# Chunk pairs of T3's inner products 0,2 with 1,3; the first half's sums all made in the gated stage; B21 of pair 0 ahead of pair 1's, with one load of a rest fewer

## The chip, the cores and the metric

The kernel runs on one core of one Trainium2 chip. The metric is the device time of one execution in microseconds (us); lower is better. A profile of one execution lies beside the times: it records when each instruction ran on each engine (PE for matrix products, DVE and ACT for elementwise work, POOL and SP for issuing transfers), what ended each wait, and what the transfers moved.

## What is computed

The reference mixes two branches of one layer with a learned gate per token (x is 2048 tokens of 640 features, the hidden width of the gated branch is 1536, there are 32 heads of 20):

```python
g = sigmoid((x * gate_w).sum(-1, keepdims=True))
a = A(x, wqkv, wo)                     # linear attention: phi(q) (phi(k)^T v) / (phi(q) . sum phi(k)), then @ wo
b = (sigmoid(x @ w_gate) * (x @ w_up)) @ w_down
return g * a + (1 - g) * b
```

The kernel folds the attention's `phi(k)^T v` and `wo` into one matrix, so that the scaled `phi(q)` and the gated hidden values are one long input of a single last product with `w_down` and that matrix stacked under each other.

## The kernel before

**Arithmetic.** Every f32 operand is split into a high and a low part (ACT writes the high part, DVE the low one: `split`), and each product of tiles is three matmuls, one at `L203` and two at `L205` (`mm3`). A matmul over 512 columns starts every 0.227 us when nothing is waited for. On top of that the products are Strassen-Winograd products of 2x2 blocks, which is where the many names come from.

**Stages.** The k projection and the attention's sums come first (to about 155 us), then the q projection, then the *gated stage* from about 222 to 513 us: a loop over `f` of 0 to 11, one block of 128 hidden features per turn, 24.5 us each, for two token pairs (pair 1 is token groups 2 and 3, pair 0 groups 0 and 1; a group has 512 tokens). Last comes the *output stage* from 513 us to the end.

**What the gated stage leaves.** For each pair it writes seven forms of the last product's input to DRAM (`h_dram[pr, name]`, names `B11 B21 T2 T1 T3 B22 T4`). Each form has 8 *chunks* of 128 rows by 512 tokens: chunks 0 to 5 come from the twelve hidden blocks (chunk `p` from `f` of `2p` and `2p+1`, stored in the turn after), chunks 6 and 7 from `phi(q)`. A ninth, shorter piece, the *rest* (`r_dram[pr]`), is left over because the length is odd.

**T3's second level.** The product with T3 is a Winograd product itself, with seven inner products P1 to P7. Its two contraction halves, A and B, are sets of chunks; `u` of 0 and 1 (the *first* and the *second half* of the sets) tells which two of the four chunks of a set are meant: `KA[u]` and `KB[u]`. Its input needs sums over DRAM, made by transfers of 512 KB that POOL issues. Those that add into their target (`accum_op`) are called *adds* below.
- `f_copy(u)`, line 1384: `f_sum` gets pair 1's A. `f_add(u, 0, KA)`, line 1387, adds pair 0's A: that is P7's input.
- `f_add(u, 0, KB)` adds pair 0's B to it in place: P6's input. `f_add(u, 1, KB)` adds pair 1's B: P3's input. As all three stand in the same place of `f_sum`, P6's add must wait until P7 has been read, and P3's until P6 has been read; `load_h` arranges that in the output stage (`F_DUE`).
- `f_low(u)`, line 1391, adds pair 0's B into its A: P5's input.

**The output stage.** `HQ` lists 62 inputs in order, each two chunks of a form (512 KB) read by SP; `jobs` runs over that list. An input takes 18, 12 or 6 matmuls (6 for an inner product), that is 4.1, 2.7 or 1.4 us. `next_h` reads into one of five raw tiles (three named `hw`, two `ws`, of which the latter also carry weights), `queue_h` splits into one of five tiles `hf`; a raw tile is free again when its split is done, and an `hf` tile when the products of the input five places before are done. The weights (`wa`; SP reads them through `ws`) are split in the same stage: kinds E, O, L, S, and I for the inner products (`("wa", "I", u)` for the two halves). The weights and inputs are put in the order of ACT and DVE by `Order`, which keeps estimated clocks of PE, ACT and DVE, and by `plan`. `load_rest(pr)` reads the rest of a pair into two tiles `ot` and splits them into `hr` (two instructions each of ACT and DVE); it is called at the places in `plan` and `REST_AT`, after so many finished inputs (`done_h`). `hr` is there once, so the rest of pair 1 takes the place of that of pair 0.

**What sets the order around the change.** SP and POOL each issue their transfers strictly in program order, and a waiting transfer holds back all behind it. In the program, a POOL transfer also waits for the landing of the POOL transfer eight places before it. In the gated stage `hooks[f]` runs once per turn, after the third step of both pairs' blocks. Tiles `c` (six with tag `c11`, six with `c12`) hold the results of a turn until POOL's stores of them have landed; ACT's first results of turn 11 take over tiles that the stores of T2 of turns 8 and 9 free.

Of the kernel before, what the change touches and what calls it, by code (L numbers as in the profile page):

```python
# [7 lines left out]
F32 = mybir.dt.float32  # L8
# [3 lines left out]
OP = mybir.AluOpType  # L12
# [3 lines left out]
P = 128  # L16
# [4 lines left out]
TG = 512  # L21
# [148 lines left out]
def a_cost(w):  # L170
    return 0.19 + w * 0.00084


def v_cost(w):
    return 0.155 + w * 0.00104
# [3 lines left out]
def gated_mix_kernel(ctx: ExitStack, tc: tile.TileContext, xt, xn, wk, wv, wo, wst_q, wst_f, out_t):  # L179
    nc = tc.nc  # L180
# [4 lines left out]
    dram = ctx.enter_context(tc.tile_pool(name="scratch", bufs=1, space=DRAM))  # L185
    order = Order()
# [10 lines left out]
    def ps_tile(tag):  # L197
        return psum.tile([P, 512], F32, name=tag, tag=tag, bufs=2)

    def mm3(out, l_hi, l_lo, r_hi, r_lo, first, last, left=False, whole=None):  # L200
        lows = [(l_hi, r_lo), (l_lo, r_hi)]
        o, r = (out, r_hi) if whole is None else whole
        nc.tensor.matmul(o, l_hi, r, start=first, stop=False, skip_group_check=True)  # L203
        for n, (a, b) in enumerate(lows[::-1] if left else lows):
            nc.tensor.matmul(out, a, b, start=False, stop=last and n == 1, skip_group_check=True)  # L205
# [51 lines left out]
    h_dram = {(pr, n): dram.tile([P, FC // 2 + 2, TG], F32, name=f"h{pr}{n}") for pr in range(2) for n in FORMS}  # L257
# [1 line left out]
    f_dram = dram.tile([P, TG], F32, name="f_dram")  # L259
    z_dram = dram.tile([32, D], F32, name="z_dram")  # L260
    s_dram = dram.tile([P, FC // 2 + 2, 2 * TG], F32, name="s_dram")
    f_sum = dram.tile([P, 4, TG], F32, name="f_sum")
    r_dram = [dram.tile([P, 2, TG], F32, name=f"r{pr}") for pr in range(2)]
    bdn = HPG * DH

# [37 lines left out]
    class XForms:  # L303
# [3 lines left out]
        def __init__(self, pool):  # L307
            self.fb, self.fr, self.fa = (self.pair(pool, *a) for a in ((3, "b"), (3, "r"), (2, "a")))
# [546 lines left out]
    for c in range(1, 4):  # L855
        ck = chunks[c]
        if c == 1:
            a, b = KPlain(2), KPlain(3)
# [15 lines left out]
        else:  # L874
            a, b = KBlock(2 * c), KBlock(2 * c + 1)
# [401 lines left out]
    for n, b in enumerate(blocks):  # L1277
        nxt = blocks[n + 1] if n + 1 < len(blocks) else None
# [98 lines left out]

    PP = (FC // 2 + 2) // 2

    KA, KB = (slice(0, 2), slice(2, 7, 4)), (slice(3, 5), slice(5, 8, 2))  # L1380
    KF = (slice(0, 2), slice(2, 4))

    def f_copy(u):
        nc.gpsimd.dma_start(f_sum[:, KF[u]], h_dram[1, "T3"][:, KA[u]])

    def f_add(u, pr, c):
        nc.gpsimd.dma_start(f_sum[:, KF[u]], h_dram[pr, "T3"][:, c[u]], accum_op=OP.add)

    def f_low(u):
        h = h_dram[0, "T3"]  # L1390
        nc.gpsimd.dma_start(h[:, KA[u]], h[:, KB[u]], accum_op=OP.add)
# [159 lines left out]
    def den_all():  # L1551
        order.need(("den", 1), False)
        queue_s()

    hooks = {0: begin, 3: den_all, 5: lambda: f_copy(0), 6: lambda: f_add(0, 0, KA), 11: lambda: f_low(0)}
    NH = 5
    WA, WI, RAW = {}, {}, {}

# [121 lines left out]
    def whole(pr, n):  # L1680
        return [(pr, n, pp) for pp in range(PP)]

    def mixed(text):

        out, at = [], {}
        for n in text.split():
            key = (1 if n.endswith("+") else 0, n.rstrip("+"))
            out.append((*key, at.get(key, 0)))
            at[key] = at.get(key, 0) + 1
        return out  # L1690

    HQ = [(pr, "B11", pp) for pp in range(PP) for pr in (1, 0)]
    HQ += whole(1, "B21") + whole(1, "T4") + whole(0, "B21")
    HQ += mixed("T2+ T2+ P7 T2+ P7 T2+ P1 T2 P1 T2 P6 T2 P6 T2 P5 P5 T1+ P2 T1+ P2 T1+ P3 P3 T1+")
    HQ += mixed("B22+ P4 B22+ P4 B22+ B22+") + whole(0, "T1") + whole(0, "B22") + whole(0, "T4")
    INNER = {"P7": (f_sum, KF), "P6": (f_sum, KF), "P3": (f_sum, KF), "P1": (h_dram[1, "T3"], KA),
             "P2": (h_dram[1, "T3"], KB), "P5": (h_dram[0, "T3"], KA), "P4": (h_dram[0, "T3"], KB)}
    F_DUE = {}
    HF, HR = {}, {}
# [7 lines left out]
    def load_h(k, tiles=None):  # L1707
        if k < len(HQ):
            pr, n, pp = HQ[k]
            if n in INNER:  # L1710
                d, c = INNER[n]
                if (n, pp) in F_DUE:
                    F_DUE.pop((n, pp))()
                src = d[:, c[pp]]
            else:
                src = h_dram[pr, n][:, 2 * pp:2 * pp + 2]
            if tiles:
                for i, t in enumerate(tiles):
                    nc.sync.dma_start(t, src[:, i])
            else:  # L1720
                if RING[k] == "hw":
                    tiles = PL["hb"].tile([P, 2, TG], F32, name="hw", tag="hw", bufs=3)
                else:
                    tiles = PL["hb"].tile([P, 2 * D], F32, name="ws", tag="ws", bufs=2)[:, :2 * TG].rearrange("p (i c) -> p i c", i=2)
                nc.sync.dma_start(tiles, src)
            HR[k] = tiles, max(order.pe, order.vec) + (5.0 if k < 5 else 8.0)
            nxt = {"P7": ("P6", 0, KB), "P6": ("P3", 1, KB)}.get(n)
            if nxt:
                key = nxt[0], pp
                F_DUE[key] = lambda: f_add(pp, *nxt[1:])  # L1730
                order.late.append((HR[k][1], lambda: F_DUE.pop(key, int)()))
# [13 lines left out]
        if k < len(HQ):  # L1745
            order.add(a_cost(2 * TG), v_cost(2 * TG), whole, ("h", k), lambda: HR[k][1] if k in HR else 1e9)

    REST, REST_AT = {}, {13: 0, 20: 1, 50: 0}
    F_AT = {20: lambda: f_low(1)}

    def load_rest(pr):

        t = [out_tile() for _ in range(2)]
        for i in range(2):
            nc.sync.dma_start(t[i], r_dram[pr][:, i])

        def fn(i):
            if i == 0:
                REST[pr] = PL["hb"].tile([P, 2, 2, TG], F32R, name="hr", tag="hr")
            split(REST[pr][:, 0, i], REST[pr][:, 1, i], t[i])  # L1760
        for i in range(2):
            order.add(a_cost(TG), v_cost(TG), lambda i=i: fn(i), ("r", pr), lambda at=order.pe + (8.0 if done_h < 13 else 11.0): at, lazy=True)

    turn = 0
    fb = {f: [FBlock(pr, f) for pr in (1, 0)] for f in range(FC)}
# [7 lines left out]
    for f in range(FC):  # L1773
        cur, nxt, old = fb[f], fb.get(f + 1, ()), fb.get(f - 1, ())
# [70 lines left out]
    def out_tile():  # L1845
        return PL["hb"].tile([P, TG], F32, name="ot", tag="ot", bufs=8)
# [8 lines left out]
    for _ in range(3):  # L1855
# [3 lines left out]
    plan = [("E", 1), ("h", 2), ("h", 3), ("E", 2), ("h", 4), ("E", 3), ("h", 5), ("O", 0),  # L1859
            ("h", 6), ("O", 1), ("h", 7), ("O", 2), ("h", 8), ("O", 3), ("h", 9), ("L", 0)]  # L1860
    plan += [("S", p) for p in range(2 * PP)] + [("I", u) for u in range(2)]
    for k in range(10, len(HQ)):
        plan.append(("h", k))
        if k == 12:
            plan.append(("r", 1))
    done_h = 0

    def advance():
# [132 lines left out]
    class Inner:  # L2001
# [3 lines left out]
        def __init__(self, n):  # L2005
            self.n = n
            if n == "P7":
                IB["t"] = ps_tile("ch")
            elif n == "P1":
                IB["u"] = ps_tile("ch")  # L2010
            x = {"P2": (1, 0), "P3": (1, 1), "P4": (0, 0)}.get(n)
            self.dst = X[x[0]][x[1]] if x else IB["u" if n in ("P1", "P5") else "t"]
            self.first = n in ("P7", "P1", "P5")

        def product(self, u, h):
            w = WI[self.n, u]
            prod(self.dst, [(w[:, 0, i], w[:, 1, i], h[:, 0, i], h[:, 1, i]) for i in (0, 1)], self.first and u == 0)

        def out(self):
            n = self.n  # L2020
# [28 lines left out]
    for k, q in jobs:  # L2049
        pr, n, pp = HQ[k]  # L2050
        if (pr, n) not in passes:
            passes[pr, n] = Inner(n) if n in INNER else Pass(pr, n)
        b = passes[pr, n]
        order.need(("h", k))
        if n in INNER:
            if q is None:
                order.need(("wa", "I", pp))
                b.product(pp, HF[k])
                if pp == 1:
                    b.out()  # L2060
        else:
            order.need(("wa", b.kind, pp))
            if b.ek == "E":
                order.need(("wa", "E2", pp))
            b.product(q, pp, HF[k])
            if pp == PP - 1:
                b.rest(q)
                b.out(q)
        if q is None:
            done_h = k + 1  # L2070
            if done_h in REST_AT:
# [54 lines left out]
```

## Time and profile before

| what | us |
|---|---|
| time, median of 3 runs (lowest, highest) | 731.04 (730.49, 731.05) |
| the profiled execution's own time | 732.2 |
| its span, first to last instruction | 730.5 |
| PE busy in the span | 719.8 |
| DVE, ACT, POOL busy | 504.1, 330.9, 139.3 |
| granted PE clock over the span | 0.999 |

The profiled execution took 1.2 us more than the median run; 1.7 us of its time lie outside the span. PE is busy for 98.5% of the span, so the figures to look for are its few waits. How to read the rows that follow: in the view over time, a row is *start, length, engine, line, operation, out<-in*, then how many instructions it merges, and in brackets how long the engine was idle before it and what ended that. In a table of windows a row has the length of the window, each engine's busy time with its instructions in parentheses, the granted PE clock, the busy share of the 16 DMA engines and what they moved in GB/s. In a list of transfer issues the last number is the median time from issue to landing in us.

### The profile page before, as it was taken

To read this page: it belongs to the slowest core of one execution; us is meant where nothing else is said; L and a number is where in the kernel's file an instruction comes from. 1 tells how busy PE (TensorE), PEld (TensorE's weight loads), DVE (VectorE), ACT (ScalarE), POOL (GpSimd) and SP (SyncE) were. 2 spreads that over 40 slices of the span, in tenths; PEclk is the share of its full clock that TensorE was granted. 3 is DMA by queue.
4 is the path that set the end of the run, shared out by engine and by line. 5 is a ranking of instruction groups with operands and counts; after the bars stand their busy time and mean duration, and the time that the engine had idled before them with its cause. 6 is when DMAs were issued, how large, how long until landed. Compare 5 with 4: busy or idle time off the path is not lost.

```text
span 730.5 us, 9634 instructions
## 1 busy us (share of the span) xinstructions
PE 719.8 (99%) x3399; PEld 605.8 (83%) x3399; DVE 504.1 (69%) x807; ACT 330.9 (45%) x563; POOL 139.3 (19%) x231
## 2 busy tenths in 40 slices
PE   9999999999999999999999999999999999899998
PEld 8998998878888888888888888888888887688786
DVE  4878576768773688678879688777768686764330
ACT  5664637267766233333333233324367565642321
POOL 0311011122530023213223222341200021010000
PEclk9999999999999999999999999999999999999999
DMA  8553535897545474556589748476988899986401
GB/s 249 138 139 72 162 55 146 206 288 253 198 159 194 152 226 130 176 195 242 215 256 327 248 182 280 174 262 207 357 276 285 297 268 294 296 281 197 166 30 72
DMA packets 64165, 152.45 MB, mean 209 GB/s; under 512 B 7887, under 2 KB 24431, under 8 KB 64118
## 3 DMA queue, kind: packets, MB, share of 16 engines
q1 hardware_dynamic: 43477, 91.65, 39.0%
q0 software_dynamic: 20496, 60.07, 27.2%
q8 instruction: 26, 0.43, 0.2%
q14 instruction: 22, 0.17, 0.1%
q10 hardware_dynamic: 144, 0.13, 0.1%
HBM read 98.20 MB, written 55.08 MB: 210 GB/s over the span
## 4 chain that ended last, share of the span: by engine, by line
PE 86%; DMA 6%; DVE 3%; ACT 3%; issue 1%; SPq 0%; DVEq 0%; ACTq 0%
PE ch L205 17%; PE rot L205 15%; PE cc L205 14%; PE dd L205 11%; PE ch L203 8%; PE rot L203 7%; PE cc L203 7%; PE dd L203 5%; DMA hw<-h0T 2%; DMA hw<-h1T 1%; ACT hf L215 1%; DMA wo_sb<-wo 1%; DMA xst<-xt 1%; DMA zacc<-kb 1%; PE rot L301 1%
## 5 line engine op out<-in xcount | busy, mean ns | idle before, releaser
L219 DVE TENSOR_TENSOR hf<-hw,hf 128x1024 fp32r<-128x1024 f32 x45 | 54.7, 1223 | 29.9 <-ACT hf L215 29.5
L219 DVE TENSOR_TENSOR c<-cc,c 128x512 f32<-128x512 f32 x56 | 37.7, 686 | 46.1 <-PE cc L205 40.5
L205 PE MATMUL ch<-hf,wa 128*128 128x512 f32 x192 | 59.3, 390 | 1.6 <-DVE hf L219 1.6
L215 ACT ACTIVATE hf<-hw 128x1024 fp32r<-128x1024 f32 x45 | 47.2, 1056 | 29.0 <-PE rot L205 20.6
L205 PE MATMUL dd<-hf,wa 128*128 128x512 f32 x144 | 44.3, 389 | 0.0
L205 PEld LDWEIGHTS ch<-hf,wa 128*128 128x128 f32 x192 | 35.8, 188 | 9.6 <-DVE hf L219 2.2
L215 ACT ACTIVATE wG<-wst 128x640 fp32r<-128x640 f32 x17 | 12.4, 737 | 65.0 <-PE dd L205 65.0
L215 ACT ACTIVATE c<-ch 128x512 f32<-128x512 f32 x32 | 19.1, 597 | 48.7 <-PE ch L205 43.9
L205 PE MATMUL rot<-hf,wa 128*128 128x512 f32 x128 | 39.4, 389 | 0.0
L203 PE MATMUL ch<-hf,wa 128*128 128x512 f32 x96 | 37.7, 393 | 0.6 <-ACT hf L215 0.4
L1849 POOL DMA_DIRECT2D out_t<-ot x18 | 9.9, 552 | 145.1 <-DVE ot L219 142.2
L203 PE MATMUL dd<-xrh,wG 128*128 128x512 f32 x90 | 35.3, 393 | 0.0
L205 PE MATMUL dd<-xrh,wG 128*128 128x512 f32 x90 | 35.1, 390 | 0.0
L205 PE MATMUL dd<-xrl,wG 128*128 128x512 f32 x90 | 35.0, 389 | 0.0
L219 DVE TENSOR_TENSOR hf<-ws,hf 128x1024 fp32r<-128x1024 f32 x15 | 18.3, 1223 | 23.2 <-ACT hf L215 23.1
L219 DVE TENSOR_TENSOR c<-c,om 128x512 f32<-128x512 f32 x48 | 33.1, 692 | 1.6
L203 PE MATMUL cc<-xbh,wS 128*128 128x512 f32 x84 | 32.7, 389 | 0.0
L205 PE MATMUL cc<-xbl,wS 128*128 128x512 f32 x84 | 32.7, 389 | 0.0
L205 PE MATMUL cc<-xbh,wS 128*128 128x512 f32 x84 | 32.7, 389 | 0.0
L205 PE MATMUL cc<-hf,wa 128*128 128x512 f32 x104 | 32.1, 390 | 0.3 <-DVE hf L219 0.3
L205 PEld LDWEIGHTS dd<-hf,wa 128*128 128x128 f32 x144 | 27.0, 188 | 5.6
L215 ACT ACTIVATE c<-rot 128x512 f32<-128x512 f32 x24 | 14.2, 597 | 38.1 <-PE rot L205 30.8
(486 smaller groups left out, 2149.0 us busy)
## 6 DMA issues: line engine op xcount, KB each, us to landing
hf<-p_dram SPq DMA_DIRECT2D x16, 512.0 KB, 4.8
wst<-wst_f SPq DMA_DIRECT2D x12, 640.0 KB, 4.6
hw<-h1T SPq DMA_DIRECT2D x13, 512.0 KB, 6.7
xst<-xt SPq DMA_DIRECT2D x10, 640.0 KB, 8.9
h1T<-c POOLq DMA_DIRECT2D x24, 256.0 KB, 3.0
h0T<-c POOLq DMA_DIRECT2D x24, 256.0 KB, 4.4
xnst<-xn SPq DMA_DIRECT2D x16, 320.0 KB, 3.2
p_dram<-qr POOLq DMA_DIRECT2D x20, 256.0 KB, 2.8
```

The source lines that it names most:

```text
L203: nc.tensor.matmul(o, l_hi, r, start=first, stop=False, skip_group_check=True)
L205: nc.tensor.matmul(out, a, b, start=False, stop=last and n == 1, skip_group_check=True)
L215: nc.scalar.activation(out, src, fn, **kw)
L219: nc.vector.tensor_tensor(out, a, b, op=op)
L301: nc.tensor.matmul(wps[:, :w], ones_w[:, :P], ones_w[:, :w], start=True, stop=True)
L1849: (eng or nc.gpsimd).dma_start(out_t[o * P:(o + 1) * P, g * TG + c0:g * TG + c1], t[:, c0:c1])
```

## The change

It has five parts.
1. The sets of chunks of T3's inner products: A was chunks 0,1 and 2,6 and B was 3,4 and 5,7; now A is 0,2 and 4,6 and B is 1,3 and 5,7. So the first half needs only chunks 0 to 3, which are there after turn 7 of the gated stage. The first half's A and B are now two strips per row rather than one.
2. `f_sum` has 8 places rather than 4: P7, P6 and P3 have places of their own for the first half, and the second half stays in one place. All adds of the first half are issued in the gated stage (`hooks` 7 to 11): P7's copy and add, two more copies of it (P6, P3), `f_low(0)`, two adds of pair 0's B, one of pair 1's B. That is two copies and one add more than before in all.
3. P7 of the second half is read before that of the first, and only the second half's adds of P6 and P3 are issued in the output stage. `f_low(1)` comes after 10 inputs rather than 20.
4. B21 of pair 0 comes ahead of B21 and T4 of pair 1. So the rest of pair 0 is needed first, then that of pair 1, then that of pair 0 again: three loads rather than four.
5. The splits of the second and the third rest are forced at a fixed place (`done_h` of 15 and 52); before, that of the third was forced only by the product that uses it.

```diff
-    f_sum = dram.tile([P, 4, TG], F32, name="f_sum")
+    f_sum = dram.tile([P, 8, TG], F32, name="f_sum")
...
-    KA, KB = (slice(0, 2), slice(2, 7, 4)), (slice(3, 5), slice(5, 8, 2))
-    KF = (slice(0, 2), slice(2, 4))
-
-    def f_copy(u):
-        nc.gpsimd.dma_start(f_sum[:, KF[u]], h_dram[1, "T3"][:, KA[u]])
-
-    def f_add(u, pr, c):
-        nc.gpsimd.dma_start(f_sum[:, KF[u]], h_dram[pr, "T3"][:, c[u]], accum_op=OP.add)
+    KA, KB = (slice(0, 3, 2), slice(4, 7, 2)), (slice(1, 4, 2), slice(5, 8, 2))
+    KF = {n: (slice(2 * i, 2 * i + 2), slice(6, 8)) for i, n in enumerate(("P7", "P6", "P3"))}
+
+    def f_copy(u, n="P7"):
+        nc.gpsimd.dma_start(f_sum[:, KF[n][u]], h_dram[1, "T3"][:, KA[u]] if n == "P7" else f_sum[:, KF["P7"][u]])
+
+    def f_add(u, pr, c, n="P7"):
+        nc.gpsimd.dma_start(f_sum[:, KF[n][u]], h_dram[pr, "T3"][:, c[u]], accum_op=OP.add)
...
-    hooks = {0: begin, 3: den_all, 5: lambda: f_copy(0), 6: lambda: f_add(0, 0, KA), 11: lambda: f_low(0)}
+    def f_copies():
+        f_copy(0, "P6")
+        f_copy(0, "P3")
+
+    def f_lows():
+        f_low(0)
+        f_add(0, 0, KB, "P6")
+        f_add(0, 0, KB, "P3")
+
+    hooks = {0: begin, 3: den_all, 7: lambda: f_copy(0), 8: lambda: f_add(0, 0, KA), 9: f_copies,
+             10: f_lows, 11: lambda: f_add(0, 1, KB, "P3")}
...
-            out.append((*key, at.get(key, 0)))
-            at[key] = at.get(key, 0) + 1
+            i = at[key] = at.get(key, -1) + 1
+            out.append((*key, 1 - i if n == "P7" else i))
...
-    HQ += whole(1, "B21") + whole(1, "T4") + whole(0, "B21")
+    HQ += whole(0, "B21") + whole(1, "B21") + whole(1, "T4")
...
-            nxt = {"P7": ("P6", 0, KB), "P6": ("P3", 1, KB)}.get(n)
+            nxt = {"P7": ("P6", 0, KB), "P6": ("P3", 1, KB)}.get(n) if pp else None
...
-    REST, REST_AT = {}, {13: 0, 20: 1, 50: 0}
-    F_AT = {20: lambda: f_low(1)}
+    REST, REST_AT = {}, {13: 1, 50: 0}
+    F_AT = {10: lambda: f_low(1)}
...
-            plan.append(("r", 1))
+            plan.append(("r", 0))
...
-            if done_h == 30:
-                order.need(("r", 1), False)
+            if done_h in (15, 52):
+                order.need(("r", int(done_h == 15)), False)
```

POOL in the gated stage, turn 10 (in these rows `h0T` with number 77 is T3 of pair 0, `f_sum` the sums; rows with `hf` are stores of the scaled `phi(q)`, rows with `c` stores of turn 9's results):

```order
 L1491 DMA h0T_75<-hf 128x512
 L1491 DMA h0T_79<-hf 128x512
+L1391 DMA h0T_77<-h0T_77 128x2x512
+L1387 DMA f_sum<-h0T_77 128x2x512 x2
 L1337 DMA h1B_85<-c 128x512
 L1337 DMA h0B_78<-c 128x512
```

Three adds now stand between the stores of `phi(q)` and the stores of turn 9, which are behind them on the same queue.

POOL at the end of the gated stage and in the output stage (`out_t<-ot` are stores of finished outputs; the rows above the first add are the last stores of T3 and T4 of pair 0):

```order
 L1337 DMA h0T_77<-c 128x512
 L1337 DMA h0T_79<-c 128x512
-L1849 DMA out_t<-ot 128x512 x3
-L1387 DMA f_sum<-h0T_77 128x1024
-L1849 DMA out_t<-ot 128x512
+L1391 DMA h0T_77<-h0T_77 128x2x512
+L1859 DMA out_t<-ot 128x512 x6
 L1387 DMA f_sum<-h0T_77 128x2x512
-L1849 DMA out_t<-ot 128x512 x2
-L1391 DMA h0T_77<-h0T_77 256x1x512
-L1387 DMA f_sum<-h1T_84 128x1024
 L1387 DMA f_sum<-h1T_84 128x2x512
```

Of five adds in the output stage three stay, and `f_low(1)` now stands ahead of the first output, right behind the last stores of the gated stage.

ACT near the end (`hr<-ot` is the split of a rest, `hf` of an input, `ot<-dd` an output of T1 of pair 0, which is the product that uses this rest):

```order
 L215 ACTIVATE ot<-rot 128x512
 L215 ACTIVATE hf<-ws 128x1024
 L215 ACTIVATE hf<-hw 128x1024
-L215 ACTIVATE hf<-ws 128x1024
-L215 ACTIVATE hf<-hw 128x1024
 L215 ACTIVATE hr<-ot 128x512 x2
+L215 ACTIVATE hf<-hw 128x1024 x2
 L215 ACTIVATE ot<-dd 128x512 x2
```

The split of the rest has moved ahead of two splits of inputs.

More of the change, by code (lines that the diff above doesn't have):

```diff
@@ L1687, in mixed @@
             key = (1 if n.endswith("+") else 0, n.rstrip("+"))
-            out.append((*key, at.get(key, 0)))
-            at[key] = at.get(key, 0) + 1
+            i = at[key] = at.get(key, -1) + 1
+            out.append((*key, 1 - i if n == "P7" else i))
         return out
     HQ = [(pr, "B11", pp) for pp in range(PP) for pr in (1, 0)]
-    HQ += whole(1, "B21") + whole(1, "T4") + whole(0, "B21")
+    HQ += whole(0, "B21") + whole(1, "B21") + whole(1, "T4")
     HQ += mixed("T2+ T2+ P7 T2+ P7 T2+ P1 T2 P1 T2 P6 T2 P6 T2 P5 P5 T1+ P2 T1+ P2 T1+ P3 P3 T1+")
     HQ += mixed("B22+ P4 B22+ P4 B22+ B22+") + whole(0, "T1") + whole(0, "B22") + whole(0, "T4")
-    INNER = {"P7": (f_sum, KF), "P6": (f_sum, KF), "P3": (f_sum, KF), "P1": (h_dram[1, "T3"], KA),
+    INNER = {**{n: (f_sum, KF[n]) for n in KF}, "P1": (h_dram[1, "T3"], KA),
              "P2": (h_dram[1, "T3"], KB), "P5": (h_dram[0, "T3"], KA), "P4": (h_dram[0, "T3"], KB)}
@@ L1761, in load_rest @@
         for i in range(2):
-            order.add(a_cost(TG), v_cost(TG), lambda i=i: fn(i), ("r", pr), lambda at=order.pe + (8.0 if done_h < 13 else 11.0): at, lazy=True)
+            order.add(a_cost(TG), v_cost(TG), lambda i=i: fn(i), ("r", pr), lambda at=order.pe + (8.0 if done_h < 14 else 11.0): at, lazy=True)
     turn = 0
@@ L2013, in __init__ @@
             self.first = n in ("P7", "P1", "P5")
+            self.done = 0
         def product(self, u, h):
             w = WI[self.n, u]
-            prod(self.dst, [(w[:, 0, i], w[:, 1, i], h[:, 0, i], h[:, 1, i]) for i in (0, 1)], self.first and u == 0)
+            prod(self.dst, [(w[:, 0, i], w[:, 1, i], h[:, 0, i], h[:, 1, i]) for i in (0, 1)], self.first and not self.done)
+            self.done += 1
         def out(self):
@@ L2058, in gated_mix_kernel @@
                 b.product(pp, HF[k])
-                if pp == 1:
+                if b.done == 2:
                     b.out()
```

## The prediction

> **What bounds the kernel now.** I read the table of windows first, then PE's rows where PE was idle, then who was late. The windows:
>
> ```profile
> 473.00:503.50 30.50, 30.50 (x136) 25.29 (x135) 23.29 (x40) 10.65 (x19) 8.57 (x16) 1.00 0.71 229
> 503.50:520.00 16.50, 16.50 (x74) 13.66 (x74) 14.70 (x24) 6.78 (x12) 7.28 (x13) 1.00 0.94 296
> 520.00:545.00 25.00, 25.00 (x112) 20.70 (x111) 16.01 (x16) 14.14 (x18) 0.40 (x1) 1.00 0.92 329
> 594.00:633.50 39.50, 37.02 (x158) 29.03 (x157) 26.26 (x32) 23.34 (x32) 5.12 (x6) 1.00 1.01 297
> ```
>
> The second number is the window, the third PE's busy time. PE is idle in the last of these windows alone, and there the DMA engines are full (1.01). The clock is 1.00 throughout. Work added to ACT or DVE costs nothing unless PE then waits, and only PE's waits can be won. PE's rows show each wait in brackets. The brackets are shorter than the loss, so I count starts: a matmul of 512 columns starts every 0.227 us, and what goes beyond that is lost.
>
> ```profile
> 614.15 0.39 PE L203 MATMUL cc<-hf,wa 128*128 128x512 f32 x1
> 614.80 0.73 PE L205 MATMUL cc<-hf,wa 128*128 128x512 f32 x2 [0.26 <-DVE hf L219]
> 615.60 0.62 PE L205 MATMUL cc<-hf,wa 128*128 128x512 f32 x2
> ...
> 625.61 0.51 PE L203 MATMUL ch<-hf,wa 128*128 128x512 f32 x1
> 626.87 0.72 PE L205 MATMUL ch<-hf,wa 128*128 128x512 f32 x2 [0.76 <-DVE hf L219]
> 633.85 0.40 PE L203 MATMUL ch<-hf,wa 128*128 128x512 f32 x1
> ...
> 688.95 0.39 PE L203 MATMUL dd<-hf,wa 128*128 128x512 f32 x1
> 690.62 0.51 PE L203 MATMUL dd<-hr,wl 128*128 128x512 f32 x1 [0.83 <-ACT hr L215]
> 692.84 0.62 PE L205 MATMUL dd<-hf,wa 128*128 128x512 f32 x2
> ```
>
> - 614.15 to 615.60: 4 starts, 0.91 us; it took 1.45. Lost 0.5.
> - 625.61 to 633.85: 21 starts, 4.76 us; it took 8.24. Lost 3.5. Here P5 and the first input of T1 of pair 1 are late.
> - 688.95 to 692.84: 7 starts, 1.59 us; it took 3.89. Lost 2.3. Here the third rest is late.
>
> Together **6.3 us**, 0.9% of the time: the most that this change can win.
>
> **Why the inputs are late at 614 and 625.** POOL's adds, and the loads around them in the list of issues (transfers, KB, us to landing):
>
> ```profile
> 584.79 0.88 POOL L1387 DMA_DIRECT2D f_sum<-h0T  x1 [18.37 <-DMA hw<-f_sum]
> 596.90 1.09 POOL L1391 DMA_DIRECT2D h0T<-h0T  x1
> 612.85 0.83 POOL L1387 DMA_DIRECT2D f_sum<-h1T  x1 [14.86 <-DMA hw<-f_sum]
> 615.55 1.16 POOL L1387 DMA_DIRECT2D f_sum<-h1T  x1 [1.88 <-DMA hw<-f_sum]
> ...
> 611.82 0.32 SPq L1725 DMA_DIRECT2D hw<-h0T  x1
> 614.77 0.32 SPq L1725 DMA_DIRECT2D ws<-h0T  x1
> 617.37 0.33 SPq L1725 DMA_DIRECT2D ws<-h1T  x1
> ...
> hw<-h0T SPq DMA_DIRECT2D x1, 512.0 KB, 4.2
> f_sum<-h1T POOLq DMA_DIRECT2D x1, 512.0 KB, 9.4
> ws<-h0T SPq DMA_DIRECT2D x1, 512.0 KB, 9.6
> ws<-h1T SPq DMA_DIRECT2D x1, 512.0 KB, 11.4
> ```
>
> The last four rows are those of the load at 611.82, the add at 612.85 and the loads at 614.77 and 617.37. The load just ahead of the add landed after 4.2 us; that just behind it (P5) after 9.6; one behind both adds (T1) after 11.4. So one add costs what is behind it 5.4 us. The second costs less: 617.37 + 11.4 = 628.8 is 4.4 us behind 614.77 + 9.6 = 624.4, and other loads moved in that time too. I take 4.5 us of the DMA engines for an add. The ends are 3.5 (those 4.4 us less one load) and 6.3 us (from the landing of the load ahead, 616.0, to the add's own, 622.3).
>
> **The change, part by part.**
>
> *Adds that leave the output stage.* Those at 584.79 and 612.85 go and that at 596.90 moves to the stage's start. Between 584 and 633 that frees 3 x 4.5 = 13.5 us of DMA time (10.5 to 18.9), and the load of a rest goes too. The loads for 614 and 625 were 0.5 and 3.5 us late. The add that stays near 613 costs 4.5 us alone, but the loads ahead of it no longer lag, and five raw and five split tiles cover about ten inputs, 20 us of PE at this place's mean of 2 us. I take the **4.0 us** as won. Next late would be the second P3's add; its reading comes some 20 us after.
>
> *The rest at the end.*
>
> ```profile
> 688.47 1.06 ACT L215 ACTIVATE hf<-hw 128x1024 fp32r<-128x1024 f32 x1 [3.02 <-PE rot L205]
> 689.43 1.13 ACT L215 ACTIVATE hr<-ot 128x512 fp32r<-128x512 f32 x2
> ```
>
> ACT's split of the rest stood behind a split that waits for PE to free a tile. Two such splits now stand behind it; each input comes every 4.1 us here, so it is done 4 us earlier. **2.3 us** won, and the two splits behind wait for their tiles anyway.
>
> *One load of a rest fewer.* Two ACT and two DVE instructions (about 1.1 and 1.3 us) stood among the splits before 614; they are part of the 0.5 there. But the second rest is now needed by B21 of pair 1:
>
> ```profile
> 569.06 0.91 SPq L1755 DMA_DIRECT2D ot<-r x2
> ...
> ot<-r SPq DMA_DIRECT2D x2, 256.0 KB, 6.0
> 564.51 0.39 PE L203 MATMUL ch<-hf,wa 128*128 128x512 f32 x1
> ```
>
> The load at the same place lands at about 575.5; ACT and DVE need 1.3 us for its first half, the one that B21 uses; PE starts B21 of pair 1 at 564.51, where it started T4 before, and comes to the rest after three inputs of 18 matmuls and one product of 6, at 564.51 + 3 x 4.08 + 1.36 = 578.1. Cover 1.3 us; cost 0, at worst 1.
>
> *P7 of the second half first.* Its weights are those split last:
>
> ```profile
> 599.71 0.69 DVE L219 TENSOR_TENSOR wa<-ws,wa 128x512 fp32r<-128x512 f32 x1
> 600.55 0.39 PE L203 MATMUL ch<-hf,wa 128*128 128x512 f32 x1
> ```
>
> That DVE instruction would end at 600.40 and PE wants them at 600.55. Cover 0.15 us; I take 0.3 lost (0 to 1).
>
> *Three adds in turn 10, two copies in turn 9, one add in turn 8.* One add in a turn happens before too (turn 6), and PE's rows show no wait after it. Three in a row do not occur. They are issued right behind the store at 473.42, and the stores of turn 9 stand behind them:
>
> ```profile
> 473.42 0.54 POOL L1491 DMA_DIRECT2D h0T<-hf  x1 [0.32 <-issue]
> 481.25 1.62 POOL L1337 DMA_DIRECT2D h1T<-c  x3 [0.20 <-issue]
> ...
> 497.39 0.60 ACT L215 ACTIVATE c<-ch 128x512 f32<-128x512 f32 x1 [4.84 <-PE ch L205]
> 500.59 0.39 PE L203 MATMUL ch<-xt2h,wV 128*128 128x512 f32 x1
> ```
>
> What lies ahead of the adds needs until about 478 (an estimate), so the DMA engines are through with them at 478 + 3 x 4.5 = 491.5 (488.5 to 497). Behind them some nine short transfers follow, of 256 KB and 0.7 us each at the third window's 329 GB/s over 0.92, until both stores of T2 have landed, near 497.5. ACT's first two results of turn 11 need those tiles. So ACT does the second of them at 497.5, then the row at 497.39, done at 498.7; PE needs that one out of `ch` at 500.59. Cover 1.9 us; cost 0 with 4.5 us an add, 3.7 with 6.3. The window of 473 to 503.5 has 0.29 x 30.5 = 8.8 us of free DMA time and takes two adds more than before (9 us), so some 1 to 2 us are carried over at most.
>
> *The start of the output stage.* `f_low(1)` waits only for the landing of T3's last store, so it goes out near 525, in a window with 2 us of free DMA time. What comes behind is up to 4 us later, with 1 to 2 us carried over.
>
> ```profile
> 519.32 1.07 POOL L1337 DMA_DIRECT2D h0T<-c  x2 [1.40 <-DVE wa L219]
> ...
> 519.09 2.36 DVE L219 TENSOR_TENSOR hf<-hw,hf 128x1024 fp32r<-128x1024 f32 x2
> 521.67 0.39 PE L203 MATMUL dd<-hf,wa 128*128 128x512 f32 x1
> ...
> 544.00 0.60 ACT L215 ACTIVATE ot<-rot 128x512 f32<-128x512 f32 x1
> 548.87 0.39 PE L203 MATMUL rot<-hf,wa 128*128 128x512 f32 x1
> ```
>
> The third input is split by 520.3 and PE wants it at 521.67: cover 1.4 us against 1 to 2. ACT empties `rot` by 544.6 behind late weights, and PE wants it at 548.87: cover 4.3 us against 4 to 5.5. I take 0.3 + 0.5 = 0.8 us lost (0 to 4).
>
> A rule of the Trainium skill bears on the first of these. "DMA: Bandwidth & Descriptors", section "Queues, rings and completion order", has each DMA engine take turns packet by packet between the queues with work, so SP's loads should pass POOL's adds. By that rule the 0.8 us would fall to nothing and the sum below be 6.0. The rows above (9.6 us behind one add against 4.2 ahead of it, and nothing landing first) are nearer to a single line, so I keep the 0.8.
>
> **The sum.** 4.0 + 2.3 won, 0.3 + 0.8 lost: 5.2 us. The profiled execution took 732.2 us, 730.5 of them its span, so it would take 727.0. It was 1.2 us slower than the median of the runs, 731.04, which gives **725.8**.
>
> **Rivals.**
> - *Half is given back.* The stores of T2 land after 500, or the output stage starts late: one of the covers of 1.9, 1.4 and 4.3 us is short by 2 to 4. For it: three adds in a row occur nowhere in this trace, and two windows have almost no free DMA time. Against: the first window has 8.8 us. Won 1.5 to 3.8: 727.2 to 729.5.
> - *The change doesn't do what it says.* The DMA engines stay full until 633 with other traffic, inputs are late again, and only the rest's 2.3 us are won, less 1 to 2 at the start: 730 to 731. Against: 13.5 us leave a stretch that is short of 3.5.
> - *Slower.* The three adds run one after the other with their whole 9.4 us each, to 474 + 28 = 502. T2's stores land near 506 after it all; ACT then empties `ch` at 507 against 500.59, some 6 us lost. The first inputs of the output stage wait for the stores behind and lose another 4. 10 lost and 6.3 won: about 735. It decides from about 8 us an add. Against it: the two adds at 612.85 and 615.55 overlapped.
>
> **How the numbers follow.** The forecast (0 to 2.4 us lost, 724.4 to 727.2 with 0.3 for the spread of the runs) has a chance of 0.56, the first rival 0.22, the second 0.12, the third 0.10. Within 0.2% is about what a measurement of this kernel can tell from no change, 729.6 to 732.5. So faster: 0.56 + 0.22 = 0.78; same 0.12; slower 0.10. The range, 724.4 to 730.5, holds the forecast, the first rival and a third of the second, and leaves out some 0.18; its upper end is where the unknown costs come to 5.8 us in place of 1.1, of the 9.7 (3.7 + 1 + 1 + 4) that their ends add up to.
>
> **What would show it.** PE's rows near 614, 625 to 633 and 690 without waits, two adds on POOL between 580 and 620, and `hr` split some 4 us ahead of PE. Against it: PE waiting for ACT at 500, for DVE's `hf` at 521 to 525, for ACT's `ot<-rot` near 549, for `hr` near 578 or for `wa` near 600. It would be wrong most of all if an add in a row of three takes over 6.3 us.

## The result, and the profile after

| | before | changed |
|---|---|---|
| median of the runs, us | 730.76 (730.06 to 731.92, 6 runs) | 724.66 (724.14 to 725.71, 6 runs) |
| ratio | 1 | 0.9917 (95%: 0.9905 to 0.9930) |
| span of the profiled execution, us | 730.5 | 723.9 |

The kernel is 6.1 us faster (5.1 to 6.9). The prediction was 725.8 within 724.4 to 730.5, a gain of 5.2 us.

The table of windows of the changed kernel (length, PE's busy time, its instructions, granted clock, share of the DMA engines, GB/s), with the bounds of the prediction's table. The changed kernel runs about 2.2 us ahead of the profile of before here, for a reason that has nothing to do with the change (point 7 below):

```profile
473.00:503.50 30.50, 30.50 (x136) 1.00 1.00 266
503.50:520.00 16.50, 16.50 (x75) 1.00 1.03 353
520.00:545.00 25.00, 25.00 (x112) 1.00 0.94 297
545.00:570.00 25.00, 23.78 (x104) 1.00 0.81 274
594.00:633.50 39.50, 39.50 (x176) 1.00 0.81 261
```

The DMA engines have moved: 0.71 to 1.00 busy in the first window, 1.01 to 0.81 in the last, where PE is now dense (it was busy for 37.02 us). One window has a gap that was not there. The waits of PE in the output stage, all that the view of waits lists:

```profile
PE ch L203 <- ACT hr L215: 1.0, 1, 1.0
PE ch L205 <- DVE hr L219: 0.2, 1, 0.2
```

The list of before has six lines there (`hf` of DVE 1.6 and 0.3 us, `hr` 0.9 and 0.8, and two more, of 0.4 and 0.2). Now only `hr` is left, once. PE's rows at that place:

```profile
556.90 0.39 PE L203 MATMUL ch<-hf,wa 128*128 128x512 f32 x1
557.13 0.61 PE L205 MATMUL ch<-hf,wa 128*128 128x512 f32 x2
558.75 0.51 PE L203 MATMUL ch<-hr,wl 128*128 128x512 f32 x1 [1.00 <-ACT hr L215]
559.47 0.74 PE L205 MATMUL ch<-hr,wl 128*128 128x512 f32 x2 [0.22 <-DVE hr L219]
560.05 0.40 PE L203 MATMUL ch<-hf,wa 128*128 128x512 f32 x1
```

By starts, six matmuls from 556.90 to 560.05 should take 1.36 us and took 3.15: **1.8 us lost**. This is B21 waiting for the first rest, the one that the plan loads behind input 12 in both kernels. ACT and the third rest, in the changed kernel's rows of ACT:

```profile
558.06 1.22 ACT L215 ACTIVATE hr<-ot 128x512 fp32r<-128x512 f32 x2 [3.61 <-DMA ot<-r]
...
675.87 1.06 ACT L215 ACTIVATE hf<-hw 128x1024 fp32r<-128x1024 f32 x1 [2.53 <-PE rot L205]
676.84 1.14 ACT L215 ACTIVATE hr<-ot 128x512 fp32r<-128x512 f32 x2
679.95 1.06 ACT L215 ACTIVATE hf<-hw 128x1024 fp32r<-128x1024 f32 x1 [1.98 <-PE rot L205]
```

The first rest is split at once when its load lands, so the load is what is late. The third is split from 676.84, and PE asks for it at 685.19 and does not wait: it was split some 7 us ahead, where the prediction had 4.

### The profile page after: what moved, and what is told of

Its sections match the earlier page's. It is cut to its first block, busy times and chain, and to the rows that moved or that the text cites. A ratio compares the mean times of both kernels' runs of the same rounds, so it can differ in the third digit from the quotient of the medians.

```text
span 723.9 us, 9626 instructions
## 1 busy us (share of the span) xinstructions
PE 718.0 (99%) x3399; PEld 605.8 (84%) x3399; DVE 503.2 (70%) x805; ACT 329.5 (46%) x561; POOL 143.2 (20%) x234
## 4 chain that ended last, share of the span: by engine, by line
PE 92%; DMA 4%; DVE 2%; ACT 1%; issue 1%; SPq 0%; ACTq 0%; DVEq 0%
PE ch L205 18%; PE rot L205 15%; PE cc L205 15%; PE dd L205 12%; PE ch L203 9%; PE rot L203 8%; PE cc L203 7%; PE dd L203 6%; DMA ws<-mp_dram 2%; DMA ws<-wst_f 1%; DVE c L219 1%; PE cc L1137 1%; DMA ot<-r 1%; PE rot L301 1%; DVE hf L219 0%
## 5 line engine op out<-in xcount | busy, mean ns | idle before, releaser
L215 ACT ACTIVATE wa<-ws 128x512 fp32r<-128x512 f32 (+2 forms) x34 | 19.8, 618 | 27.2 <-DMA ws<-wst_f 11.6
L219 DVE TENSOR_TENSOR wa<-ws,wa 128x512 fp32r<-128x512 f32 (+2 forms) x34 | 22.3, 680 | 14.2 <-ACT wa L215 13.9
```

Source lines behind the costliest of these rows:

```text
L215: nc.scalar.activation(out, src, fn, **kw)
L219: nc.vector.tensor_tensor(out, a, b, op=op)
```

## The experiments

All times are medians. A ratio is to runs of the kernel before that were made beside the run, whose medians lie between 730.55 and 731.28, so ratios compare better than times. "Lost" is what PE's starts beyond 0.227 us, waits and slow matmuls together, come to in the output stage of the run's one profile.

| run | what | us | ratio to before (95%) | lost, us |
|---|---|---|---|---|
| before, profile shown above | | 730.76 | 1 | 6.4 |
| changed | | 724.66 | 0.9917 (0.9905 to 0.9930) | 1.8 |
| e1_wide | before, `f_sum` wider | 729.62 | 0.9983 (0.9972 to 0.9994) | 6.2 |
| e2_rest52 | before, third rest forced | 728.00 | 0.9966 (0.9953 to 0.9980) | 4.5 |
| e3_low20 | changed, `f_low(1)` late | 724.30 | 0.9916 (0.9900 to 0.9932) | 0.3 |
| e4_adds_back | changed, first half's sums late | 725.42 | 0.9937 (0.9920 to 0.9953) | 2.0 |
| e5_again | changed, again | 724.96 | 0.9905 (0.9884 to 0.9925) | 1.3 |
| e6_rest_early | changed, first rest earlier | 724.28 | 0.9898 (0.9877 to 0.9919) | 0.3 |
| e7_six_adds | changed, three adds more | 730.89 | 0.9991 (0.9976 to 1.0006) | 6.5 |
| e8_no52 | changed, third rest not forced | 726.73 | 0.9926 (0.9904 to 0.9949) | 5.2 |
| e9_rest_late | changed, third rest late | 729.56 | 0.9982 (0.9967 to 0.9997) | 5.3 |
| e10_early_p7 | e6 with P7's old order | 724.23 | 0.9906 (0.9889 to 0.9923) | 0.0 |
| e11_all | e10 with `f_low(1)` late | 724.11 | 0.9921 (0.9890 to 0.9953) | 0.0 |
| e12_before_again | before, again | 730.21 | 0.9997 (0.9983 to 1.0011) | 5.3 |

### The third rest: one part alone, and the rest without it

```diff
 e2_rest52, from the kernel before
-            if done_h == 30:
-                order.need(("r", 1), False)
+            if done_h in (30, 52):
+                order.need(("r", int(done_h == 30)), False)
 e8_no52, from the changed kernel
-            if done_h in (15, 52):
+            if done_h == 15:
```

> The kernel before with one edit of the change alone: the split of the third rest is forced when the input 51 is done. Theory: it takes away the wait of 2.3 us at 688.95 to 692.84 and nothing else, 730.8 - 2.3 = 728.5, and hr is split some 4 us ahead of PE. Rival: the two splits that now stand behind it are late instead, and the time stays at 730.8.

> The changed kernel without the forced split of the third rest. The wait of 2.3 us at 690 comes back. With f_sum widened alone the profile showed more there: behind the wait the granted clock was 0.50 for 3 us and the matmuls took 1.6 us longer. Theory: the wait lets the clock drop in a part of the runs: those with a mean granted clock of 1.000 take 727.0, those with 0.998 take 728.6, and the median lies between. Rival: the lower clocks come from elsewhere: 727.0 with clocks like those of the changed kernel beside it.

Alone it won 2.5 us (1.5 to 3.4), and its profile has no wait for `hr`. Taken out of the changed kernel it cost 1.8 us against e5_again beside it, and its profile has the wait again and more. The granted clock behind it, in windows of e8_no52:

```profile
684.00:686.00 2.00, 0.98 (x4) 1.00 0.25 100
686.00:688.00 2.00, 1.27 (x4) 0.87 0.00 0
688.00:690.00 2.00, 2.00 (x6) 0.50 0.00 0
690.00:692.00 2.00, 2.00 (x8) 0.78 0.35 131
```

PE is busy all through 688 to 690 and gets through 6 records in place of 10: the clock is at 0.50. Starts give 2.3 us lost in the wait and 1.6 more in the slow matmuls behind it. That run took 728.9; the five others of the kernel, with a mean clock of 0.999 or 1.000, took 725.9 to 727.3. So the theory's two times came out, 728.9 with the lower clock and 727 or less without, but by one run of six, and such a run can be chance; e9_rest_late below tests it with more.

### The first half's sums

```diff
 e4_adds_back, from the changed kernel
-    KF = {n: (slice(2 * i, 2 * i + 2), slice(6, 8)) for i, n in enumerate(("P7", "P6", "P3"))}
+    KF = {n: (slice(0, 2), slice(6, 8)) for i, n in enumerate(("P7", "P6", "P3"))}
-    hooks = {0: begin, 3: den_all, 7: lambda: f_copy(0), 8: lambda: f_add(0, 0, KA), 9: f_copies,
-             10: f_lows, 11: lambda: f_add(0, 1, KB, "P3")}
+    hooks = {0: begin, 3: den_all, 7: lambda: f_copy(0), 8: lambda: f_add(0, 0, KA), 10: lambda: f_low(0)}
-            nxt = {"P7": ("P6", 0, KB), "P6": ("P3", 1, KB)}.get(n) if pp else None
+            nxt = {"P7": ("P6", 0, KB), "P6": ("P3", 1, KB)}.get(n)
```

> The changed kernel with the sums of the first half (P6's and P3's) made in the output stage again, as before: two adds near 590 and 615 come back, three adds and two copies leave turns 9 to 11. Theory: the 4.0 us around 614 and 625 were short by little; with f_low of the second half out of it the two adds need 5.4 to 9 us of the DMA engines and the two stretches have some 8.9 us free, so at most 1 us is lost there, and the relief of turn 10 may win back part of the 1.8 us: 723 to 725.7. Rival: the 4.0 us hang on just these adds: 728.7 with PE waiting at 614 and 625 again.

Neither theory: PE lost 2.0 us, at P5, where the profile of before lost most; the time, 725.42, lies in the range of the first. PE's rows of e4_adds_back, and its windows:

```profile
623.79 0.39 PE L203 MATMUL ch<-hf,wa 128*128 128x512 f32 x1
625.69 0.73 PE L205 MATMUL ch<-hf,wa 128*128 128x512 f32 x2 [1.51 <-DVE hf L219]
```

```profile
473.00:503.50 30.50, 30.50 (x137) 1.00 0.68 213
594.00:633.50 39.50, 37.99 (x167) 1.00 0.90 265
```

A share of 0.90 over the whole window still hides two adds at 606.97 and 610.20, three microseconds apart and just ahead of P5's loads. The reverse case is e3_low20, further down: there `f_low(1)` is at its old place and the first half's sums are made early, and PE loses nothing at 614 to 633. So the sums of the first half are what this stretch was short of, and moving `f_low(1)` out of it was not needed in the profiles of e3 and e11. On the other side the 1.8 us at 557 are gone, with `f_low(1)` where the change puts it. So the two halves of this edit nearly cancel in a profile, 2.0 against 1.8 us.

### The wait for the first rest

```diff
 e3_low20
-    F_AT = {10: lambda: f_low(1)}
+    F_AT = {20: lambda: f_low(1)}
 e6_rest_early
-        if k == 12:
+        if k == 11:
             plan.append(("r", 0))
```

> The changed kernel with f_low of the second half put back to where it stood before (after input 19 in place of input 9). The changed kernel's PE waits 1.8 us at 557 to 560 for the split of the first rest. Theory: f_low at 521.64 holds up the loads of the output stage's start, so without it the rest is in time and the add is hidden later, where the DMA engines are 0.81 busy: 724.7 - 1.8 = 722.9. Rival: the adds of turns 10 and 11 do it, which leave the DMA engines full from 473 to 520: the wait stays, 724.7, or up to 726 where f_low then costs something at 600 to 630.

> The changed kernel once more, unchanged: a second profile of it. In its first profile PE waits 1.8 us at 557 to 560 for the first rest; moving f_low away took that wait out of the profile (0.3 us lost in all), yet the median moved by 0.4 us only (724.3 against 724.7). If the wait is steady, it shows again with 1.5 to 2.1 us. If it is luck of the DMA engines, this profile shows less than 1 us and the time is that of the run without it, 724.3 +- 0.4.

> The changed kernel with the load of the first rest put one input earlier into the plan (behind input 11 in place of 12). If the wait at 557 is there in most runs, the rest lands some 4 us earlier, the wait goes and the time falls by up to 1.8 us, to 722.9. If the wait is there in few runs, the time is that of the changed kernel run beside it within 0.5 us.

With `f_low(1)` moved, with the load of the rest moved, or (e4) with the adds taken out of turns 9 to 11, the one profile of the run has no wait there. But the wait comes and goes without any edit too. Four profiles have the first rest as the change has it: PE lost 1.8 us there in the first, 0.7 in e5_again, 0.9 in e8_no52 and nothing in e9_rest_late (the edits of the last two act on the third rest alone, over 100 us later). Five profiles with one of the edits (e3, e4, e6, e10, e11) all lost nothing. So that the wait needs both the adds and `f_low(1)` is likely but not shown, and it is a matter of little. By e5_again's expectation, less than 1 us, it is luck of the transfers; its time of 724.96 lies just above the 724.3 +- 0.4 given for that. The 722.9 that e3_low20 and e6_rest_early hoped for did not come: the medians are 724.30 and 724.28 without the wait, 724.66 and 724.96 with it, which the intervals don't separate. e5_again also lost 0.5 us at the second rest, and e8_no52 0.3.

How the add reaches the rest, in the list of issues: the load of one input of B11 (`hw<-h0B`; transfers, KB, us to landing). Before, issued at 523.56:

```profile
hw<-h0B SPq DMA_DIRECT2D x1, 512.0 KB, 7.4
```

The same load in the changed kernel, issued at 521.23:

```profile
hw<-h0B SPq DMA_DIRECT2D x1, 512.0 KB, 11.3
```

`f_low(1)` was issued at 521.64, 0.4 us *behind* this load, and still the load took 3.9 us longer. Not all of the 3.9 us is its doing, since the time varies without it. This is the load in e3_low20, where the adds of turns 7 to 11 stay and only `f_low(1)` is gone from here:

```profile
hw<-h0B SPq DMA_DIRECT2D x1, 512.0 KB, 8.4
```

Over all profiles but e7's the load took 10.4 to 11.3 us in the seven with `f_low(1)` beside it (e4, without most of the adds, among them) and 7.4 to 8.6 us in the six without. So `f_low(1)` alone costs it some 2 to 4 us, and the earlier adds cost it nothing that shows. In a single line, with the load ahead, it would cost nothing, so the queues share the DMA engines, as the rule that the prediction quotes from the Trainium skill says ("DMA: Bandwidth & Descriptors", "Queues, rings and completion order"); what the prediction drew from the rule, that the loads lose nothing, does not follow. The weights behind are late (their third pair is issued at 533.91, in e3_low20 at 530.70), ACT splits them in a fixed order, and SP's row of the rest's load shows what has built up by then. In the changed kernel:

```profile
551.63 0.84 SPq L1765 DMA_DIRECT2D ot<-r  x2
```

And before:

```profile
549.79 0.90 SPq L1755 DMA_DIRECT2D ot<-r  x2
```

It is issued 1.8 us later although PE is 2.2 us earlier: 4.0 us between these two profiles, against a cover of 3.5. But they are the two ends. In the three other profiles with the old order (e1, e2, e12), where PE is not late, it is issued at 549.30 to 549.96 and the cover is 0.6 to 1.5 us; in the three others of the changed order (e5, e8, e9) it is issued at 549.84 to 550.21, and e9 still has 0.8 us of cover; in e3 and e4 it is issued at 548.60 and 548.69. The rest's own load varies as well, from 5.8 to 7.0 us over these profiles. The cover was short from the start, and a delay of a microsecond or two uses it up.

### The price of an add, with more of them in a row

```diff
 e7_six_adds, from the changed kernel
-    f_sum = dram.tile([P, 8, TG], F32, name="f_sum")
+    f_sum = dram.tile([P, 14, TG], F32, name="f_sum")
 in f_lows, behind the three adds of turn 10
+        for i in range(3):
+            nc.gpsimd.dma_start(f_sum[:, 8 + 2 * i:10 + 2 * i], h_dram[0, "T3"][:, KB[0]], accum_op=OP.add)
 in turn 7, behind f_copy(0)
+        for i in range(3):
+            nc.gpsimd.dma_start(f_sum[:, 8 + 2 * i:10 + 2 * i], h_dram[1, "T3"][:, KA[0]])
```

> The changed kernel with three more adds of 512 KB right behind the three of turn 10, into scratch that nobody reads (and three copies of 512 KB in turn 7 that fill it). It prices an add where several stand in a row. In the changed kernel the three landed at 481.32, 484.05 and 486.68, 2.7 us apart, and the two stores of T2 behind them at 488.59 and 490.45; ACT then ran 0.95 us later than before and PE waited for nothing. With 2.7 us an add the stores land 8.1 us later, the second at 498.5; ACT empties ch at 499.7 against PE's 498.4, and PE loses 1 to 2 us near 498 and up to 2 more behind it: 726 to 728.5. With the 4.5 us of the prediction, 13.5 us later: PE loses 6 to 7 us near 498, 731 or more. With adds that run beside the stores and cost nothing: 724.7.

The changed kernel's list of issues (us to landing last), first the add that was issued at 471.64:

```profile
h0T<-h0T POOLq DMA_DIRECT2D x1, 512.0 KB, 9.7
```

and the two issued at 472.40 and 473.12, with the middle of both:

```profile
f_sum<-h0T POOLq DMA_DIRECT2D x2, 512.0 KB, 12.6
```

The first landed at 481.3, the two behind at 485.4 in the middle: 2.7 us from one to the next. ACT's first row behind T2's store in the changed kernel:

```profile
488.69 0.60 ACT L215 ACTIVATE c<-dd 128x512 f32<-128x512 f32 x1 [5.89 <-DMA h1T<-c]
```

The same row in e7_six_adds:

```profile
496.29 0.60 ACT L215 ACTIVATE c<-dd 128x512 f32<-128x512 f32 x1 [13.37 <-DMA h1T<-c]
```

7.6 us for three, 2.5 us each. The six adds themselves landed at 480.6, 483.4, 485.9, 488.6, 491.1 and 494.3, 2.5 to 3.2 us apart. The three further ones were issued at 480.80, 483.78 and 486.29, each 0.2 to 0.4 us behind the landing of the add three places before it, and the stores behind them had to wait for that on POOL; the profile names no reason for these waits. The whole cost was 5.9 us against e5_again, more than the 1 to 4 expected, and none of it near 498, where it was expected. The view of waits of e7_six_adds:

```profile
PE cc L203 <- DVE c L219: 1.2, 1, 1.2
PE dd L205 <- DVE hf L219: 1.1, 2, 0.9
PE ch L203 <- ACT hr L215: 1.1, 1, 1.1
PE ch L205 <- DVE hf L219: 0.6, 1, 0.6
PE ch L205 <- DVE hr L219: 0.5, 2, 0.2
PE rot L203 <- ACT ot L215: 0.4, 1, 0.4
PE dd L203 <- ACT hf L215: 0.3, 1, 0.3
```

The first stands at 504.91, in turn 11; then the third input at 521.84, `rot` near 551, the first rest at 563 and the second at 583. The covers that the prediction lists are used up one after the other, since the backlog passes on through the full windows. So the path of the prediction's slower rival is there, but it took six adds to go that way, and the kernel was then about as fast as before (0.9991, 0.9976 to 1.0006), not slower.

### The base, and the clock

```diff
 e1_wide, from the kernel before
-    f_sum = dram.tile([P, 4, TG], F32, name="f_sum")
+    f_sum = dram.tile([P, 8, TG], F32, name="f_sum")
 e9_rest_late, from the changed kernel
-    REST, REST_AT = {}, {13: 1, 50: 0}
+    REST, REST_AT = {}, {13: 1, 53: 0}
-            if done_h in (15, 52):
+            if done_h in (15, 53):
```

> The kernel before with the scratch tensor f_sum eight slots wide instead of four and nothing else: only addresses move. The profile of before has a wait of PE of 2.2 us at 155.84 (for a result that ACT copies late behind a late load of wo), long ahead of all that the change touches; that of the changed kernel has none. If that wait is luck of the DMA engines, the time is that of before, 730.8 +- 0.5, and the profile may show the wait or not. If the new addresses remove it, the time is 728.6 and the profile shows no wait there.

> The kernel before, unchanged, against itself: a control and a second profile. With f_sum widened alone the time was 0.9983 of before (0.9972 to 0.9994), 0.9 us less, and its profile had no wait at 155.84. If the wider tensor does that by its addresses, this run's ratio is 1.000 +- 0.001 and its profile shows the wait of 2.2 us at 155.84, or that wait is luck and the 0.9 us stay unexplained. If the ratio is 0.998 again, the 0.9 us lie in how the two sets of runs compare, and not in the kernel. In the output stage this profile should lose 6.2 us as the two before it did, or 4.6 to 4.7 where the clock does not drop behind the wait for the third rest.

> The changed kernel with the third rest loaded behind input 52 in place of 49 and split at once. It makes PE's wait for hr near 687 longer than the 2.3 us that it was before. Theory: what lowers the granted clock is such a wait, and a longer one does it in more runs: with a wait of 3 us or more the profile shows 0.50 for about 3 us behind it, most runs have a mean clock of 0.998 or less, and the time is that of the changed kernel, 724.8, plus the wait, plus 1.6: about 729 to 731. Rival: the clock falls by chance: most runs at 0.999 to 1.000 as in the changed kernel, and the time is 724.8 plus the wait alone.

PE's wait of 2.2 us at 155.84 stands in the first profile of before and in none of the thirteen others, e12_before_again among them, which is the same kernel: luck. e1_wide's time lies between its two expectations. By the ratios the wider `f_sum` gave 1.2 us (0.4 to 2.0), the kernel before against itself 0.2 us (-0.8 to 1.2); those intervals overlap, and whether addresses give anything stays open. In the output stage e12_before_again lost 5.3 us, between its expected 6.2 and 4.7, at a clock of 1.00.

In e9_rest_late PE lost 3.7 us at the third rest, and its windows show the clock again:

```profile
684.00:686.00 2.00, 0.00 (x0) 1.00 0.56 213
686.00:688.00 2.00, 1.34 (x5) 1.00 0.00 0
688.00:690.00 2.00, 2.00 (x7) 0.57 0.00 0
690.00:692.00 2.00, 2.00 (x7) 0.57 0.35 131
692.00:694.00 2.00, 2.00 (x10) 1.00 0.03 8
```

Seven of its 12 runs have a mean clock of 0.998 or less and took 729.3 to 731.8, the five others 727.6 to 728.5. Of the 80 runs of the kernel before for which the clock was recorded, 37 have 0.998 or less (median 731.5) and 43 more (730.1). Of the 12 runs of the changed kernel none has, and of 26 of its versions without the wait for the third rest (e3, e4, e6, e10, e11) one. So the rival, the clock by chance alone, is hard to hold: seven of 12 against none of 12. That a longer wait does it in more runs is not shown, since seven of 12 and 37 of 80 are too close. Nor is it this one wait alone: e2_rest52 has one such run of six, and e7_six_adds four of 12, with the third rest in time and shorter waits elsewhere.

### What is left

```diff
 e10_early_p7 is e6_rest_early with
-            out.append((*key, 1 - i if n == "P7" else i))
+            out.append((*key, i))
 e11_all is e10_early_p7 with
+    F_AT = {20: lambda: f_low(1)}
```

> The changed kernel with the first rest loaded one input earlier and P7's halves in their old order. Theory: the 0.3 us that PE loses near 598 in two of the profiles is the wait for the weights that are split last, which P7's second half asks for first; with the old order it goes and the output stage loses 0 to 0.1 us in the profile; the time falls by up to 0.3 us against the run without this edit, 724.28, which the measurement can hardly tell. Rival: the wait at 598 is for something else and stays.

> The changed kernel with the first rest loaded one input earlier, P7's halves in their old order and f_low of the second half after input 19. Theory: nothing is left that PE waits for in the output stage, in the profile and in the other runs: 724.0, with a smaller spread than the changed kernel. Rival: f_low among the loads of 600 to 630 costs something again: 724.3 to 725.

The 0.3 us near 598 in the profiles of e3 and e6 are gone in both, and PE loses less than 0.05 us in the output stage. The time is that of e3 and e6, 724.1 to 724.3, with nothing left in this stage to win from waits. e11's spread was not smaller (one of its six runs took 731.24 at a clock of 0.995; no profile shows where that run lost it).

## Why the prediction was right, point by point

1. **What bounds the kernel** (6.3 us at three places, the most to win): the places were right, the size in part luck. With nothing lost in the stage the time was 724.1 to 724.2, 6.5 us under before. But the size at 614 to 633 is one profile's: 4.0 us there, and 2.3, 2.9 and 4.5 in the three other profiles with the old adds (e1, e12, e2). Their mean is 3.4, which with the 2.3 of the rest makes 5.7; the other 0.8 is the clock (point 3), which the prediction did not have.
2. **Adds that leave the output stage, 4.0 won**: right; PE's rows there have no wait. In e4's profile the first half's two adds are worth 2.0 of it, and e3 and e11 show that `f_low(1)`, the third add of the prediction's 13.5 us, could have stayed.
3. **The rest at the end, 2.3 won**: the mechanism was right, the size too small. The wait was 2.3 us in every profile that had it (e9, which makes it longer, aside), but it also lowers the granted clock in a part of the runs, for 1.6 us more in each of the three profiles that show it (e1, e8, e9). The shortfall of the mean clock times the span is 1.0 us over the 80 runs of before and 0.2 over the 12 of the changed kernel (the record gives the clock to 0.001, which is 0.7 us in a single run).
4. **P7 of the second half first, 0.3 lost**: right in size where it shows (0.3 in e3 and e6, gone with the old order). It shows in two of the seven profiles that have the new order (e7 aside); what decides that is open.
5. **The start of the output stage, 0.8 lost**: the step that failed. "What comes behind is up to 4 us later" held (2 to 4 us at the load of B11, some 0 to 2 at that of the first rest), but the two places that it names, the third input and `rot`, kept their cover. The loss was 1.8, 0.7, 0.9 and 0.0 us in four profiles, at the first rest, which the list of covers left out because its load and its use had not changed place. The prediction's reason for keeping the 0.8, that the rows are nearer to a single line, does not hold up either: the load that was slowed had been issued ahead of the add. That 0.8 lies so near the mean of these four losses is luck.
6. **Three adds in turn 10 and the second rest, nothing lost**: right (0.5 and 0.3 us at the second rest in two of four profiles), though with a price of 4.5 us an add, which is 2.7 in a row. ACT's row came 0.95 us later than before, and its cover held. At six adds it did not.
7. **The base**: the profiled execution lay 1.2 us above the median and had lost 2.2 us to luck. The sum of the terms by the changed kernel's two profiles, 6.4 less 1.8 or 1.3, is 4.6 to 5.1 us; the clock gives 0.8 more, 5.4 to 5.9, against 6.1 (5.1 to 6.9) measured. With means of four profiles on either side (3.4 + 2.3 lost before; 1.8, 1.3, 1.2 and 0.0 after, e8 and e9 without their third rest) it is 5.7 - 1.1 + 0.8 = 5.4 us; the difference to 6.1 is within the interval. The prediction's 5.2 came near by luck: a size of 4.0 that was above the mean stood against a clock that it did not have.
8. **The bounds**: the first rival's 1.5 to 3.8 us won does not come out of its own terms, a cover short by 2 to 4 us, which taken from the 5.2 leave 1.2 to 3.2. The measured time lies in the forecast either way.

## What to carry to other kernels

When work is moved off a full stretch, list as covers not only what changes its place but everything that the moved transfers can delay downstream, loads of small operands first; the one left out was the one that ran late. Move only what the stretch needs to lose: here `f_low(1)` could have stayed. Price a wait of PE of some 2.3 us, the shortest that a profile here shows with the low clock behind it, with what the clock may do. And take the sizes of waits from more than one profile where two can be had: here the same wait came to 2.3 to 4.5 us.

## What the runs showed of the hardware

- A wait of 2.3 us, in two pieces of 0.8 and 0.9 us idle around one record, was enough to halve the granted clock for about 3 us: windows of e1_wide with PE busy 0.50 of 2 us, and then a clock of 0.66 and 0.50. Added up over the windows (at half the clock, twice the clock's shortfall in each), the slow stretch is 3.4 us long in e1_wide, e8_no52 and e9_rest_late alike. The same wait in the profile of e12_before_again left it at 1.00. The Trainium skill ("TensorE: Matmul & The Clock Gate", "Part 1: The HAM clock gate") has the clock fall after an idle window of some 3.4 us that runs freely. The length of the slow stretch and the chance from run to run agree with it; the shorter wait does not. The windows of e1_wide:

```profile
686.00:688.00 2.00, 0.50 (x1) 1.00 0.02 8
688.00:690.00 2.00, 1.95 (x6) 0.66 0.00 0
690.00:692.00 2.00, 2.00 (x6) 0.50 0.24 90
```

- Adds of 512 KB in a row landed 2.5 to 3.2 us apart (e7_six_adds), while one alone took 7.9 us from issue to landing (the add at 612.10 of the changed kernel).
- The same load of 512 KB by SP took 7.4 to 8.6 us in six profiles without an add on POOL's queue beside it, and 10.4 to 11.3 us in seven with one, although it was issued ahead of it.
